# A fused FFT and mixture-of-experts kernel: the first two batches routed in halves, pauses between weight instructions on VectorE, and sums over partitions in bfloat16

## The chip, the cores and the metric

One core of a Trainium2 chip runs the whole program in one launch. The metric is the device time of that launch in microseconds, the median of several executions. The engines are named as the profile names them: PE (TensorE) multiplies matrices and PEld loads its weights, DVE (VectorE), ACT (ScalarE), POOL (GpSimd) and SP (SyncE) do the rest; each takes its instructions strictly in the order in which they stand in its queue.

## The reference

The input `x` is 8 batches of 2496 tokens by 256 features. Its two-dimensional Fourier transform, real part, is the input of a layer of 8 experts: each token goes to the expert with the largest logit.

```python
X = np.fft.fft(np.fft.fft(x, axis=1), axis=2).real      # 8 x 2496 x 256
x = X.reshape(19968, 256)
logits = x @ w_gate + modality_bias[modality_id]
e_idx = np.argmax(logits, axis=1)
gate_w = softmax(logits)[arange, e_idx]
for e in range(8):
    mask = e_idx == e
    h = np.maximum(x[mask] @ w1[e], 0.0)                 # 256 -> 1024
    out[mask] = gate_w[mask, None] * (h @ w2[e])         # 1024 -> 256
```

## The kernel before, in words

**Transform.** Each batch is loaded (`XM`, L368) and folded by DVE and ACT, goes through the three products of the transform on PE (`stage1` L523 or L520 in fp32 or fp16 form, `stage23` L554 or L549 and L569 or L567), and comes out of `evac` (L500 on ACT, L501 on DVE) as rows of 516 values in tiles `rp` of three groups of 128 tokens (`CH` = 3). A batch has 11 groups (`G` = 11). Half of the spectrum is enough: the mirrored rows `rm` are made from `rp` with a copy and a change of sign (`Group.rows`, L215, L217, L218). `Lg` (L577) collects the logits of each group.

**Routing.** `route(b)` (L609 to L684) runs on DVE behind the last group of a batch: logits, maximum, one-hot code, rank of each token within its expert (two kinds of small PE products, L653 and L655, and a running base `nbase`), and the destination `dsti` (L666). It works on all 22 columns (11 groups and their 11 mirrors) at once. It is a generator; the strings `ORDER0`, `ORDER1` give in which order its steps (`r`) alternate with steps of the next batch's `stage1` (`s`) and folds (`f`, `F`). The first three `r` steps have raised priority. The last of them makes the rows and for batches 0 and 1 issues at once their 22 indirect DMAs (`scatter`, L687, on POOL), which put each row at its place in `xd`, sorted by expert.

**Experts.** A block is 128 or 256 tokens of one expert. SP fetches it transposed (`xT`, L1038), PE makes the first product (L1054), ACT and DVE square off its two halves into `H` (L1059, L1060), PE makes the second product (L1072), ACT scales it (`ob`, L1078) and POOL writes it to its rows of the output with two indirect DMAs (L1079). The first three blocks (experts 0, 1, 2) are run as soon as batch 0 is in `xd`, 13 more when batch 1 is (`ORDER_S`); the rest follow batch by batch.

**Weights.** The fp32 weights of each expert (two units `u` per expert) are loaded (`wload`, L793), folded (L801, L802), measured (`wnorm`, L815, L817, L400), rounded to a scaled fp16 upper part by ACT (`whi`, L836) and a lower part by DVE (`wlo`, L843, four instructions of 128x1024 per expert), and stored (`wstore`, L851). `fft_moe` places these parts among the steps of the transform by hand with `steps(n)` and `behind(f, ins)`, the second at raised priority.

**Sums over partitions.** The scales are powers of two, taken from sums of squares: `total` (L400) multiplies a column of sums by a matrix of fp32 ones, `pow2` (L386 to L388) makes the power of two and its inverse.

**What sets the order.** A scheduler orders the instructions once, when the program is built, by priority, by `issue_after` and by the places where the source writes them; pools of tiles (`rt.tile(..., bufs=n)`) make a writer wait until the readers of the slot it takes over are done. Tiles `rp` of batches 0 to 2 have 6 slots (`RPB`), tiles `rm` 2 (`RMB`).

Of the kernel before, what the change touches and what calls it, by code (L numbers as in the profile page):

```python
# [34 lines left out]
RPB = 6  # L35
# [11 lines left out]
RMB = 2  # L47
# [39 lines left out]
ORDER1 = "rrrrrrrfssssFssss"  # L87
# [111 lines left out]
class Group:  # L199


    def __init__(self, k, b, g0, rp, tail, dsti):
# [31 lines left out]
class Kernel:  # L234
    def __init__(self, ctx, tc, t):
# [46 lines left out]
        self.ones = c.tile([P, P], F32, name="ones")  # L282
# [112 lines left out]
    def total(self, st, ps):  # L395
# [136 lines left out]
    def stage23(self, b):  # L532
# [8 lines left out]
        for g in range(G + 1):  # L541
# [67 lines left out]
    def route(self, b):  # L609
        nc, t, rt = self.nc, self.t, self.rt  # L610
        V, bc, be, tc = nc.vector, self.bc, self.be, self.tc
        Lg = self.Lg
        L = rt.tile([P, NC, 8], F32, name="L")
        V.tensor_tensor(L[:, 0:G, :], Lg[:, :, 0], Lg[:, :, 1], ALU.add)
        V.tensor_tensor(L[:, G:NC, :], Lg[:, :, 0], Lg[:, :, 1], ALU.subtract)
# [654 lines left out]
```

## Time and profile before

| what | us |
|---|---|
| three executions | 1132.57, 1125.27, 1128.35 |
| median | 1128.35 |
| the profiled execution | 1134.3 |
| its span, first to last instruction | 1132.5 |
| PE busy in it | 1028.2 |
| DVE busy in it | 561.6 |

All positions below are microseconds from the start of that span. A row of a timeline is start, duration, engine, line, operation, output and inputs, tile and count, and in brackets the idle time of the engine before it with what ended it. "Remote" and "another core or an unknown queue" stand for a signal whose sender the profile does not name; "issue" is idle time in which nothing shown was waited for. A row of the chain is start, duration and what ran or was waited for.

### The profile page before, as it was taken

The numbers are of one execution on the slowest core, as the hardware profiler recorded it, in microseconds if no ns is written. First come the engines' busy times: TensorE is split into PE (matmuls) and PEld (weight loads), VectorE is DVE, ScalarE is ACT, GpSimd is POOL, SyncE is SP. The second block draws the span as 40 slices with busy tenths as digits, with TensorE's granted clock in tenths as the row PEclk, the third lists the DMA queues.
The fourth block names the chain that finished last, engine by engine and source line by source line (L and its number), as shares of the span: only waits on it lengthen the run. The fifth ranks groups of instructions, "written<-read, shape, count | busy, mean of one in ns | idle before, by whom it ended". The sixth has DMA issues, their size and how long they took to land.

```text
span 1132.5 us, 26026 instructions
## 1 busy us (share of the span) xinstructions
PE 1028.2 (91%) x9980; PEld 913.4 (81%) x9980; DVE 561.6 (50%) x1645; ACT 441.0 (39%) x870; POOL 365.6 (32%) x351
## 2 busy tenths in 40 slices
PE   7954699987998699899999999999999999999997
PEld 6843489876897488698788989888888888899896
DVE  3638486968676368666456434642222222322231
ACT  4724174846552254443344333332232332323232
POOL 0156611146313232433433343244533221222111
PEclk9987799999999689899999999999999999999999
DMA  9465391668667568267766767388769898486963
GB/s 335 151 257 162 141 293 44 226 213 264 190 184 234 178 197 271 75 179 219 232 209 178 212 196 233 76 224 264 229 171 285 261 248 251 120 255 164 262 150 80
DMA packets 150011, 229.73 MB, mean 203 GB/s; under 512 B 116341, under 2 KB 117407, under 8 KB 132727
## 3 DMA queue, kind: packets, MB, share of 16 engines
q1 hardware_dynamic: 133319, 185.85, 57.3%
q0 software_dynamic: 16560, 42.15, 10.6%
q8 instruction: 80, 1.31, 0.5%
q14 instruction: 52, 0.43, 0.1%
HBM read 198.08 MB, written 62.48 MB: 230 GB/s over the span
## 4 chain that ended last, share of the span: by engine, by line
PE 61%; issue 14%; DVE 7%; DMA 6%; ACT 4%; another core or an unknown queue 4%; POOL 2%; ACTq 1%; SPq 0%; POOLq 0%; DVEq 0%
PE pso L1072 27%; PE psm L1054 26%; PE psf L549 2%; DMA XM<-x 2%; PE psf L567 2%; POOL out L1079 2%; DMA out<-ob,ig 2%; PE psf L554 1%; ACTq L1078 1%; PE psf L520 1%; DVE H L1060 1%; DVE w L843 1%; DMA pack<-c_pack 1%; DMA xd<-rm,dsti 1%
## 5 line engine op out<-in xcount | busy, mean ns | idle before, releaser
L1054 PE MATMUL psm<-xT,w 128*128 128x256 f16 (+1 forms) x4368 | 464.8, 263 | 35.9 <-issue 11.7
L1072 PE MATMUL pso<-w,H 128*128 128x256 f16 x3864 | 466.4, 276 | 20.5 <-issue 10.3
L1054 PEld LDWEIGHTS <-w 128*128 128x128 f16 x4368 | 386.6, 99 | 83.1 <-issue 38.3
L1072 PEld LDWEIGHTS <-H 128*128 128x128 f16 x3864 | 379.2, 99 | 73.5 <-issue 26.9
L1060 DVE SCALAR_TENSOR_TENSOR H<-psm,H 128x512 f16<-128x512 f32 x322 | 219.2, 686 | 299.4 <-ACT H L1059 244.2
L1079 POOL DMA_INDIRECT out<-ob,ig x161 | 162.1, 1007 | 625.7 <-ACT ob L1078 596.7
L1059 ACT ACTIVATE H<-psm 128x512 f16<-128x512 f32 x322 | 189.5, 597 | 280.8 <-PE psm L1054 199.7
L1078 ACT ACTIVATE ob<-pso,gs 128x256 f32<-128x256 f32 x161 | 69.4, 472 | 246.6 <-PE pso L1072 163.0
L687 POOL DMA_INDIRECT xd<-rp,dsti x88 | 102.8, 1169 | 84.1 <-ACT T L496 50.1
L687 POOL DMA_INDIRECT xd<-rm,dsti x88 | 92.0, 1045 | 48.5 <-issue 30.1
L501 DVE SCALAR_TENSOR_TENSOR T<-psf,T 120x280 f16<-120x280 f32 (+2 forms) x114 | 51.4, 462 | 56.3 <-ACT T L500 55.1
L500 ACT ACTIVATE T<-psf 120x280 f16<-120x280 f32 (+2 forms) x114 | 46.6, 424 | 38.2 <-PE psf L549 11.1
L1075 DVE TENSOR_SCALAR gs<-ig,w 128x2 f32<-128x2 f32 (+1 forms) x91 | 20.2, 223 | 72.3 <-DMA ig<-xd 44.6
L567 PE MATMUL psf<-T,pack 120*128 120x145 f16 (+1 forms) x396 | 41.5, 227 | 3.5 <-issue 1.6
L549 PE MATMUL psf<-pack,T 128*120 128x144 f16 (+1 forms) x396 | 40.2, 235 | 3.4 <-issue 3.1
L549 PEld LDWEIGHTS <-T 128*120 128x120 f16 x396 | 33.2, 137 | 3.6 <-issue 2.3
L567 PEld LDWEIGHTS <-pack 120*128 120x128 f16 x396 | 30.4, 99 | 7.1 <-issue 4.1
L501 DVE SCALAR_TENSOR_TENSOR rp<-psf,rp 128x256 f16<-128x256 f32 x66 | 27.4, 415 | 14.1 <-ACT rp L500 13.0
L520 PE MATMUL psf<-c,XM 128*128 128x132 f16 x360 | 28.7, 223 | 5.3 <-issue 3.3
L500 ACT ACTIVATE rp<-psf 128x256 f16<-128x256 f32 x66 | 25.3, 389 | 17.7 <-PE psf L567 11.0
L843 DVE SCALAR_TENSOR_TENSOR w<-wa,wsc,w 128x1024 f16<-128x1024 f32 x24 | 29.9, 1277 | 4.2 <-ACT w L836 4.2
L520 PEld LDWEIGHTS <-XM 128*128 128x128 f16 x360 | 23.9, 99 | 7.4 <-issue 4.1
(203 smaller groups left out, 621.2 us busy)
## 6 DMA issues: line engine op xcount, KB each, us to landing
w<-w SPq DMA_DIRECT2D x83, 1028.0 KB
w<-w SPq DMA_DIRECT2D x83, 1024.0 KB
XM<-x SPq DMA_DIRECT2D x14, 1280.0 KB
wa<-w SPq DMA_DIRECT2D x16, 1024.0 KB
out<-ob,ig POOLq DMA_INDIRECT x161
XM<-x SPq DMA_DIRECT2D x2, 768.0 KB
xT<-xd SPq DMA_TRANSPOSE x91
xd<-rp,dsti POOLq DMA_INDIRECT x88
```

The lines of the kernel that those rows point to most:

```text
L500: self.acted = self.nc.scalar.activation(dst[:, 0], ps, AF.Identity, scale=scale).ins
L501: self.mark = self.nc.vector.scalar_tensor_tensor(dst[:, 1], ps, scale, dst[:, 0], ALU.mult, ALU.subtract).ins
L520: nc.tensor.matmul(o, src[:, a, i0 + i, :], self.c1h[:, w, i1 + i, :], start=k == 0, stop=k == 2)
L549: nc.tensor.matmul(oh, T1[h][:, a, g, :], self.m2h[h][:, w], start=h + k == 0, stop=h * k == 2, skip_group_check=True)
L567: nc.tensor.matmul(ps3[0:P, cols], self.e3h[:, a, j, :], T2[:, w, cols], start=k == 0, stop=k == 2)
L687: i = self.nc.gpsimd.indirect_dma_start(out=self.t["xd"], out_offset=bass.IndirectOffsetOnAxis(ap=at, axis=0), in_=row, in_offset=None, bo ...
L1054: l1 = nc.tensor.matmul(ps[:, q, :], w1v[:, h, kt, ft], xT[:, xs, :], start=k == 0, stop=k == 5).ins
L1059: nc.scalar.activation(H[:, 0, f0:f0 + NF, :], ps, AF.Relu)
L1060: self.mark = V.scalar_tensor_tensor(H[:, 1, f0:f0 + NF, :], ps, 0.0, H[:, 0, f0:f0 + NF, :], ALU.max, ALU.subtract).ins
L1072: nc.tensor.matmul(po[:, tg, :], H[:, hh, ft, tg * P:(tg + 1) * P], w2v[:, wh, ft, :], start=k == 0, stop=k == 23)
L1078: self.ob = nc.scalar.activation(ob, po[:, tg, :], AF.Identity, scale=gs[:, tg:tg + 1]).ins
L1079: ins = nc.gpsimd.indirect_dma_start(out=t["out"], out_offset=bass.IndirectOffsetOnAxis(ap=ig.bitcast(I32)[:, tg, 0:1], axis=0), in_=ob, i ...
```

## The change

1. **Sums.** The ones are bfloat16. `total` multiplies the upper 16 bits of each fp32 sum, taken as bfloat16, and `pow2` multiplies the result by 1.01.
2. **Halves.** `route(b, ga, gb)` works on groups `ga` to `gb`. For batches 0 and 1 (`RH` = 2) it is called for groups 0 to 5 while `stage23` still makes groups 6 to 10 (three steps at group 6, then one for each group), and for groups 6 to 10 behind them. `ORDER0` and `ORDER1` have five `r` in place of seven, and two `steps` in `fft_moe` are shorter by two.
3. **Row tiles.** `rp` and `rm` of batches 0 to 2 share 8 slots.
4. **Pauses.** Behind each of the two low-part instructions of units 0 to 5 (`NG` = 6) `breathe` asks for four clears of one element per partition (`gap`, on 64 partitions), each to issue after the one before: 48 clears.

```diff
-RPB = 6
+RPB = 8
-RMB = 2
-ORDER0 = "rrrrrrrfssssFssss"
+ORDER0 = "rrrrrfssssFssss"
-ORDER1 = "rrrrrrrfssssFssss"
+ORDER1 = "rrrrrfssssFssss"
+RH = 2
+GH = 6
+RN0 = 3
+RG0 = 0
+NG = 6
+TR = 1.01
...
-    def __init__(self, k, b, g0, rp, tail, dsti):
+    def __init__(self, k, b, g0, rp, tail, dsti, ga, n):
+        self.c = [s * n + g0 - ga for s in range(2)]
...
-        pool, n = (k.rt, RMB) if self.b < SPB else (k.rows, RML)
-        rp, rm = rows = self.rp, pool.tile([P, CH, RW], I16, name="rm", bufs=n)
+        pool, n = (k.rt, RPB) if self.b < SPB else (k.rows, RML)
+        rp, rm = rows = self.rp, pool.tile([P, CH, RW], I16, name="rm", tag="row" if self.b < SPB else "rm", bufs=n)
...
+        self.gap = pk[64:P, 872:873]
-        self.ones = c.tile([P, P], F32, name="ones")
+        self.ones = c.tile([P, P], BF16, name="ones")
...
-        V.tensor_scalar(eb, ss, m, 1e-34, ALU.mult, ALU.max)
+        V.tensor_scalar(eb, ss, m * TR, 1e-34, ALU.mult, ALU.max)
...
-            nc.tensor.matmul(ps[:, 0:1], self.ones, st[:, i:i + 1], start=i == 0, stop=i == n - 1)
+            nc.tensor.matmul(ps[:, 0:1], self.ones, st.bitcast(BF16)[:, 2 * i + 1:2 * i + 2], start=i == 0, stop=i == n - 1)
...
-                    self.rp.append(pool.tile([P, CH, RW], I16, name="rp", bufs=n))
+                    self.rp.append(pool.tile([P, CH, RW], I16, name="rp", tag="rp" if pool is self.rows else "row", bufs=n))
...
-    def route(self, b):
+    def route(self, b, ga=0, gb=G):
+        n = gb - ga
+        m = 2 * n
...
-        nbase = rt.tile([P, 8], F32, name="nbase")
+        nbase = rt.tile([P, 8], F32, name="nbase", bufs=4)
...
-        self.base = self.bases[b + 1] = nbase
+        self.base = nbase
...
-        self.ntok += N
-        self.nbat = b + 1
+        if gb == G:
+            self.bases[b + 1] = nbase
+            self.ntok += N
+            self.nbat = b + 1
...
+                if b < RH and g >= GH:
+                    if g == GH:
+                        r = self.route(b, 0, GH)
+                        for _ in range(RN0):
+                            with self.hp(HR[min(b, 1)]):
+                                next(r)
+                    elif g > GH + RG0:
+                        next(r, None)
+            if b < RH:
+                for _ in r:
+                    pass
-            r, nr = self.route(b), 0
+            r, nr = self.route(b, GH) if b < RH else self.route(b), 0
...
+    def breathe(self, i):
+        for _ in range(4):
+            with self.tc.issue_after(i.ins):
+                i = self.nc.vector.memset(self.gap, 0.0)
...
-            V.scalar_tensor_tensor(o[:, 2 * F + m * i:2 * F + m * i + m], x, s, o[:, m * i:m * i + m], ALU.mult, ALU.subtract)
+            i = V.scalar_tensor_tensor(o[:, 2 * F + m * i:2 * F + m * i + m], x, s, o[:, m * i:m * i + m], ALU.mult, ALU.subtract)
+            if u < NG:
+                self.breathe(i)
...
-    steps(7)
+    steps(5)
     behind(both(k.wlo, 0, 1), k.head)
...
-    steps(4)
+    steps(2)
     behind(both(k.wlo, 4, 5), k.head)
```

What this does to the order of three places follows (a row is line, operation, output and inputs, shape, and a count where it repeats; lines of the new kernel are higher by some 20 to 40).

On POOL before, from the first scatter to the first writes of a block's output: the rows of batch 0 (22 scatters), of batch 1 (22), then block 0.

```order
L687 DMA xd<-rp,dsti 162048x516 x6
L687 DMA xd<-rm,dsti 162048x516 x3
L687 DMA xd<-rp,dsti 162048x516 x3
L687 DMA xd<-rm,dsti 162048x516 x3
L687 DMA xd<-rp,dsti 162048x516 x2
L687 DMA xd<-rm,dsti 162048x516 x5
L687 DMA xd<-rp,dsti 162048x516 x9
L687 DMA xd<-rm,dsti 162048x516 x3
L687 DMA xd<-rp,dsti 162048x516 x2
L687 DMA xd<-rm,dsti 162048x516 x8
L1079 DMA out<-ob,ig_1120 19968x256 x2
```

And now:

```order
L707 DMA xd<-rp,dsti 162048x516 x6
L707 DMA xd<-rm,dsti 162048x516 x6
L707 DMA xd<-rp,dsti 162048x516 x5
L707 DMA xd<-rm,dsti 162048x516 x5
L707 DMA xd<-rp,dsti 162048x516 x3
L707 DMA xd<-rm,dsti 162048x516 x3
L707 DMA xd<-rp,dsti 162048x516 x3
L707 DMA xd<-rm,dsti 162048x516 x3
L1117 DMA out<-ob,ig_1248 19968x256 x2
L707 DMA xd<-rp,dsti 162048x516 x5
L707 DMA xd<-rm,dsti 162048x516 x5
```

The rows come half by half, and the two output writes of block 0 have moved ahead of the last ten scatters of batch 1.

On DVE before, around the low parts of expert 0 (`w_0`):

```order
L891 SCALAR_TENSOR_TENSOR sp_nd_3_1104<-sp_ok_3_1096,done_99 1x3
L843 SCALAR_TENSOR_TENSOR w_0_104<-wf,wsc,w_0_104 128x1024
L843 SCALAR_TENSOR_TENSOR w_0_104<-wa,wsc,w_0_104 128x1024
L843 SCALAR_TENSOR_TENSOR w_0_107<-wa,wsc,w_0_107 128x1024 x2
L845 MEMSET w_0_107 128x7
L846 TENSOR_TENSOR w_0_107<-web 128x1
L600 TENSOR_TENSOR bias<-bias,btmp 128x176
```

And now:

```order
L929 SCALAR_TENSOR_TENSOR sp_nd_3_1232<-sp_ok_3_1224,done_99 1x3
L879 SCALAR_TENSOR_TENSOR w_0_104<-wf,wsc,w_0_104 128x1024
L839 MEMSET pack 64x1
L665 TENSOR_SCALAR tail<-gate,xinv 128x10
L879 SCALAR_TENSOR_TENSOR w_0_104<-wa,wsc,w_0_104 128x1024
L879 SCALAR_TENSOR_TENSOR w_0_107<-wa,wsc,w_0_107 128x1024 x2
L607 TENSOR_TENSOR bias<-bias,btmp 128x176
L394 TENSOR_SCALAR xeb<-xeb 128x1
L922 TENSOR_SCALAR sp_st_3_1226<-sp_st_3_1226 1x8
L883 MEMSET w_0_107 128x7
L884 TENSOR_TENSOR w_0_107<-web 128x1
```

One of the clears (MEMSET of `pack`, the tile that holds `gap`) and the last step of the first tail stand behind the first low part; the other three low parts stand back to back as before, and the clears that belong to them come later.

On DVE before, between batch 1's destinations and the low parts of expert 1 (`w_1`):

```order
L215 COPY rp<-tail 128x3x2
L215 COPY rm<-tail 128x3x2
L215 COPY rp<-tail 128x3x2
L217 COPY rm<-rp 128x3x2x129
L218 TENSOR_SCALAR rm<-rp 128x3x2x127
L215 COPY rp<-tail 128x2x2
L217 COPY rm<-rp 128x3x2x129
L218 TENSOR_SCALAR rm<-rp 128x3x2x127
L380 TENSOR_TENSOR XM<-XM 128x1280 x2
L843 SCALAR_TENSOR_TENSOR w_1_105<-wf,wsc,w_1_105 128x1024
L843 SCALAR_TENSOR_TENSOR w_1_105<-wa,wsc,w_1_105 128x1024
L843 SCALAR_TENSOR_TENSOR w_1_108<-wa,wsc,w_1_108 128x1024 x2
```

And now, between the second half's ranks of batch 1 and the same low parts:

```order
L1098 SCALAR_TENSOR_TENSOR H_1250<-psm,H_1250 128x512
L682 SCALAR_TENSOR_TENSOR dst<-pack,dst 128x10
L1098 SCALAR_TENSOR_TENSOR H_1250<-psm,H_1250 128x512
L917 TENSOR_SCALAR sp_ok_13_1735<-sp_av_1731 1x8
L660 TENSOR_REDUCE gate<-L 128x10
L917 TENSOR_SCALAR sp_ok_13_1747<-sp_av_1731 1x8
L684 CAST dsti<-dst 128x10
L387 TENSOR_TENSOR XM<-XM 128x1280 x2
L605 TENSOR_TENSOR bias<-mf,mb 128x176
L606 TENSOR_TENSOR btmp<-mid,mb 128x176
L879 SCALAR_TENSOR_TENSOR w_1_105<-wf,wsc,w_1_105 128x1024
L839 MEMSET pack 64x1
```

The copies for the mirrored rows no longer stand ahead of `XM` and `w_1`, and three of the `H` instructions of block 0 (L1098, before L1060; the first of the three stands a few rows higher) have moved ahead of them and of the destinations `dsti` of batch 1's second half.

## Rows read from the trace of the kernel before

**Rows 1.** The page, busy time and count of the engines, and the span in 40 slices of 28.3 us (busy tenths of PE, the granted clock of PE in tenths of full speed, the busy tenths of the DMA engines).

```profile
PE 1028.2 (91%) x9980; PEld 913.4 (81%) x9980; DVE 561.6 (50%) x1645; ACT 441.0 (39%) x870; POOL 365.6 (32%) x351
...
PE   7954699987998699899999999999999999999997
...
PEclk9987799999999689899999999999999999999999
DMA  9465391668667568267766767388769898486963
```

**Rows 2.** Windows: stretch, its length, busy time and count of PE, PEld, DVE, ACT, POOL, the granted clock of PE, the DMA share and GB/s.

```profile
68.00:81.00 13.00, 1.12 (x5) 0.62 (x4) 0.87 (x4) 1.20 (x4) 7.80 (x8) 0.74 0.63 242
81.00:93.00 12.00, 6.73 (x31) 5.37 (x32) 7.88 (x34) 7.09 (x12) 2.78 (x3) 0.78 0.09 31
93.00:102.00 9.00, 0.93 (x9) 0.67 (x8) 7.03 (x28) 1.98 (x4) 7.33 (x6) 0.50 0.43 106
102.00:135.00 33.00, 22.93 (x192) 18.68 (x191) 21.39 (x62) 7.05 (x13) 26.60 (x22) 0.81 0.63 212
...
250.00:300.00 50.00, 41.10 (x370) 35.37 (x369) 36.62 (x79) 32.59 (x53) 27.14 (x22) 0.97 0.84 251
900.00:1000.00 100.00, 100.00 (x918) 89.62 (x917) 28.25 (x50) 31.22 (x59) 19.46 (x20) 1.00 0.74 212
```

**Rows 3.** The timeline of PE.

```profile
80.72 1.30 PE L569 MATMUL psf<-T,pack 120*128 120x145 f32 x4 [11.88 <-ACT T L496]
...
101.36 5.78 PE L1054 MATMUL psm<-xT,w 128*128 128x256 f16 x36 [8.07 <-DMA xT<-xd]
...
274.95 2.21 PE L1054 MATMUL psm<-xT,w 128*128 128x256 f16 x12 [2.84 <-DVE H L1060]
```

**Rows 4.** The timeline of POOL.

```profile
51.21 1.12 POOL L687 DMA_INDIRECT xd<-rp,dsti  x1 [49.77 <-ACT T L496]
52.63 5.90 POOL L687 DMA_INDIRECT xd<-rp,dsti  x1 [0.30 <-ACT T L496]
...
77.09 0.97 POOL L687 DMA_INDIRECT xd<-rp,dsti  x1 [0.30 <-issue]
89.61 0.97 POOL L687 DMA_INDIRECT xd<-rm,dsti  x1 [11.55 <-DVE L L617]
...
94.75 0.97 POOL L687 DMA_INDIRECT xd<-rm,dsti  x1 [0.30 <-issue]
...
132.42 0.98 POOL L687 DMA_INDIRECT xd<-rm,dsti  x1 [0.30 <-issue]
133.70 0.98 POOL L1079 DMA_INDIRECT out<-ob,ig  x1 [0.30 <-issue]
```

**Rows 5.** The timeline of SP's queue.

```profile
98.02 0.70 SPq L1038 DMA_TRANSPOSE xT<-xd  x1
```

**Rows 6.** The timeline of DVE.

```profile
37.00 0.16 DVE L577 COPY Lg<-psf 128x16 f32<-128x16 f32 x1
...
43.27 0.25 DVE L614 TENSOR_TENSOR L<-Lg 128x88 f32<-128x88 f32 x1
...
43.72 0.34 DVE L617 TENSOR_TENSOR L<-L,bias 128x176 f32<-128x176 f32 x1
...
50.11 0.15 DVE L666 CAST dsti<-dst 128x22 int32<-128x22 f32 x1
...
53.69 3.66 DVE L843 SCALAR_TENSOR_TENSOR w<-wa,wsc,w 128x1024 f16<-128x1024 f32 x3
...
57.30 0.06 DVE L845 MEMSET w<- 128x7 uint32 x1
...
88.14 0.15 DVE L215 COPY rm<-tail 128x6 int32<-128x6 int32 x1
...
122.24 0.16 DVE L215 COPY rm<-tail 128x6 int32<-128x6 int32 x1 [1.52 <-DMA xd<-rm,dsti]
...
128.53 0.17 DVE L215 COPY rm<-tail 128x4 int32<-128x4 int32 x1 [4.86 <-DMA xd<-rm,dsti]
...
133.99 0.16 DVE L386 TENSOR_SCALAR web<-psf 128x1 f32<-128x1 f32 x1 [4.07 <-remote]
134.18 0.15 DVE L387 TENSOR_SCALAR web<-web 128x1 int32<-128x1 int32 x1
...
138.30 0.29 DVE L817 SCALAR_TENSOR_TENSOR wj<-psf,eye 128x128 bf16<-128x128 f32 x1 [3.59 <-remote]
```

**Rows 7.** Two stretches of the chain that ended last.

```profile
119.62 2.31 DMA xd<-rm,dsti
...
260.06 6.81 DMA xd<-rm,dsti
...
268.25 5.02 issue
```

**Rows 8.** The timeline of ACT.

```profile
130.49 0.84 ACT L1078 ACTIVATE ob<-pso,gs 128x256 f32<-128x256 f32 x2 [6.51 <-remote]
```

**Rows 9.** Windows of line L400 alone: stretch, its length, busy time and count of PE and of PEld, the clock, the DMA share and GB/s.

```profile
170.00:620.00 450.00, 8.68 (x60) 9.12 (x60) 0.94 0.64 194
```

**Rows 10.** Groups of line L400 by form, and the page's group of the fp16 weight loads of the experts' second product: for the first, count and the least, median and greatest ns of one, and the first and last start; for the second, count, busy time and mean ns of one.

```profile
L400 PEld LDWEIGHTS psf<-wst,ones x40: 190/192/338, 190.5 to 306.6; 128*128 128x128 f32 x40
...
L1072 PEld LDWEIGHTS <-H 128*128 128x128 f16 x3864 | 379.2, 99 | 73.5 <-issue 26.9
```

More of the change, by code (lines that the diff above doesn't have):

```diff
@@ L607, in be @@
         return v.unsqueeze(1).to_broadcast([P, NC, 8])
-    def route(self, b):
+    def route(self, b, ga=0, gb=G):
         nc, t, rt = self.nc, self.t, self.rt
[L611 to L615, printed above, removed]
+        V, tc = nc.vector, self.tc
+        n = gb - ga
+        m = 2 * n
+        two = lambda x: x.rearrange("p (s g) -> p s g", s=2)[:, :, ga:gb]
+        bc = lambda v: v.unsqueeze(2).to_broadcast([P, m, 8])
+        be = lambda v: v.unsqueeze(1).to_broadcast([P, m, 8])
+        by2 = lambda x: x.rearrange("p (s g) e -> p s g e", s=2)
+        Lg = self.Lg[:, ga:gb]
+        L = rt.tile([P, NC, 8], F32, name="L")[:, 0:m]
+        V.tensor_tensor(L[:, 0:n, :], Lg[:, :, 0], Lg[:, :, 1], ALU.add)
+        V.tensor_tensor(L[:, n:m, :], Lg[:, :, 0], Lg[:, :, 1], ALU.subtract)
+        bs = by2(self.bs)[:, :, ga:gb]
@@ L623, in route @@
         V.tensor_tensor(eq, L, bc(mx), ALU.is_equal)
         V.tensor_tensor(eq, eq, be(self.misc[:P, 8:16]), ALU.mult)
-        ix = rt.tile([P, NC], F32, name="ix")
+        ix = rt.tile([P, NC], F32, name="ix")[:, 0:m]
         V.tensor_reduce(ix, eq, AX.X, ALU.min)
-        V.scalar_tensor_tensor(ix, self.misc[:P, 24:46], 64.0, ix, ALU.mult, ALU.add)
+        bad = two(self.misc[:P, 24:46])
+        ix2 = ix.rearrange("p (s g) -> p s g", s=2)
+        V.scalar_tensor_tensor(ix2, bad, 64.0, ix2, ALU.mult, ALU.add)
@@ L642, in route @@
         yield
[L643 removed]
+        gate = rt.tile([P, NC], F32, name="gate")[:, 0:m]
         V.tensor_reduce(gate, L, AX.X, ALU.add)
@@ L652, in route @@
         o4f = o4.rearrange("p c e -> p (c e)")
-        nc.tensor.matmul(ps[:, 0:176], self.tri[:, 0, :], oh.rearrange("p c e -> p (c e)"), start=True, stop=False, skip_group_check=True)
-        for j in range(1, NC + 1, 4):
-            nc.tensor.matmul(ps[:, 8 * j:184], self.tri[:, 1, :], o4f[:, 0:184 - 8 * j], start=False, stop=j + 4 > NC, skip_group_check=True)
-        rk = rt.tile([P, NC, 8], F32, name="rk", bufs=1)
-        V.tensor_tensor(rk, ps[:P, 0:176].rearrange("p (c e) -> p c e", e=8), be(self.base[:P, :]), ALU.add)
@@ L658, in route @@
-        nbase = rt.tile([P, 8], F32, name="nbase")
-        V.tensor_tensor(nbase, ps[:, 176:184], self.base, ALU.add)
-        self.base = self.bases[b + 1] = nbase
+        w = 8 * m + 8
+        nc.tensor.matmul(ps[:, 0:8 * m], self.tri[:, 0, :], oh.rearrange("p c e -> p (c e)"), start=True, stop=False, skip_group_check=True)
+        for j in range(1, m + 1, 4):
+            nc.tensor.matmul(ps[:, 8 * j:w], self.tri[:, 1, :], o4f[:, 0:w - 8 * j], start=False, stop=j + 4 > m, skip_group_check=True)
@@ L672, in route @@
         yield
-        for i, g0 in enumerate(range(0, G, CH)):
-            group = Group(self, b, g0, self.rp[i], tail, dsti)
+        for g0 in range(ga, gb, CH):
+            group = Group(self, b, g0, self.rp[g0 // CH], tail, dsti, ga, n)
             if b < 2:
@@ L680, in route @@
             else:
-                self.pend += [(group, n) for n in range(2 * group.gn)]
-            if b == B - 1 and i == 3:
-                self.pend += [(self.pad, n) for n in range(E)]
+                self.pend += [(group, i) for i in range(2 * group.gn)]
+            if b == B - 1 and g0 == 9:
+                self.pend += [(self.pad, i) for i in range(E)]
             yield 1
```

37 lines of the change are left out of this document (20 added, 17 removed).

## The prediction

> **What bounds the kernel now**
>
> I read the page first. PE is busy for 1028.2 of 1132.5 us and its slices stand at 9 from the middle on, but there are holes in the first third [rows 1]. The windows put numbers on this: from 900 to 1000 us PE is busy for 100.00 of 100, while 68 to 81 holds 1.12 of 13, 81 to 93 6.73 of 12, 93 to 102 0.93 of 9, 102 to 135 22.93 of 33 and 250 to 300 41.10 of 50 [rows 2]. PE idles there for 11.88, 5.27, 8.07, 10.07 and 8.90 us. So the end is set by PE's work, and an edit gains only what it takes from these holes or from PE's work itself.
>
> Next I looked for what ends each hole. Three timelines answer for the early ones. PE waits 11.88 us to 80.72, then 8.07 us to 101.36 for the first fetched rows (DMA xT) [rows 3]. SP issues that fetch at 98.02 [rows 5], 3.27 us after the last scatter of batch 0 left POOL at 94.75 [rows 4]. That scatter is late because POOL idled 11.55 us before 89.61: the mirrored rows it needs are made on DVE from 88.14 [rows 6], behind batch 1's last row. From 102 to 138 DVE waits: 1.52 and 4.86 us for slots of `rm`, 4.07 and 3.59 us for a signal the profile calls remote [rows 6]. The chain has a landing of 2.31 us under the first wait, one of 6.81 us at 260, and 5.02 us of waiting before 273.27 [rows 7].
>
> **The change part by part**
>
> The sum is made against the profiled execution, 1134.3 us, which is 5.95 above the median of 1128.35; I take that off at the end.
>
> *Start of block 0.* Group 5's logits are ready at 37.00 against 43.27 for the start of routing now; routing then takes 6.84 us to `dsti` at 50.11 [rows 6]. So first destinations come at about 43.9 and the first scatter at 44.4, not 51.21. At the pitch of 1.28 us (132.42 to 133.70) and with the 4.9 us that one scatter lost (5.90 for about 1) [rows 4], twelve are out by 44.4 + 11 x 1.28 + 4.9 = 63.4, and ten more by 76.2. With the 6.61 us from the last scatter to PE's start now (94.75 to 101.36) block 0 could start at 82.8; PE has batch 1's transform to finish first, which ends at about 88 now, so I take 88, or 13.4 us earlier. Not all of this reaches the end. The work DVE does from 81 to 135 is 7.88 + 7.03 + 21.39 = 36.3 us of 54 [rows 2], which stays; only its 17.7 us of waits can go. Bounds 0 and 13.4; I take 4, about a third, because DVE's other work between 88 and 101 stays and now shares the engine with block 0's `H`.
>
> *Row slots.* With 8 shared slots the two waits for `rm`, 1.52 and 4.86 us, should go: gain 0 to 6.4, I take 5. Next late is then POOL itself, whose scatters are back to back. Batch 2's 5.02 us before 273.27 go in the same way, but only 2.84 us of that is PE idle (before 274.95) [rows 3]: 0 to 5, I take 3. Against that stands that `rp` now queues for the same slots; with all 22 scatters out by 76 it finds them free, and a wait there lies in the next item.
>
> *The hole from 68 to 81.* Nothing in the change removes its cause, which the rows leave unnamed. Scatters run through it now and will then. Some of PE's work may move across it: 0 to 5, I take 2.
>
> *The late signals, 4.07 and 3.59 us.* They sit in a run of scatters which now ends earlier. 0 to 7.7; I take half of it, 3.5.
>
> *Sums.* Line L400 holds PE for 8.68 us in 60 records between 170 and 620, 0.145 each [rows 9]. A sum is two such records and should become one, with a weight load of 99 ns as the page shows for fp16 in place of 192 [rows 10]. That is 30 x 0.145 = 4.3 us of PE, part of it inside holes: 0 to 8.7, I take 2.5.
>
> *Added work on DVE.* The trace has no chain of clears. A clear costs 0.06 us by the one at 57.30, or 0.19 by the pitch of instructions that wait for each other (133.99 to 134.18) [rows 6]: 48 cost 3 to 9 us. Halving a wide step costs 2 x 0.25 instead of 0.34 (43.27, 43.72), some 13 times in each of two batches, 4.2 us, and about as many short ones at 0.15 double, 4 us more. Most lies where DVE waits for ACT or PE, above all around 68 to 80: the run of clears stands there. Bounds 0 and -11 for what reaches the path; I take -5. `pow2` keeps its number of instructions: nothing.
>
> A scatter that normally takes 1 us took 5.90 beside the three low-part instructions at 53.69 [rows 4, 6]. The Trainium skill ("GPSIMD Engine Reference", section "Key points") says that GpSimd shares its SBUF interfaces with VectorE and contends with instructions that have two SBUF inputs, as these have; this trace agrees, with that 5.90. By that rule the pauses would give up to 4.9 us back to POOL. But the order puts one clear behind the first low part only, and three still run back to back, so I count none.
>
> Sum: 4 + 5 + 3 + 2 + 3.5 + 2.5 - 5 = 15 us. 1134.3 - 15 = 1119.3; on the median's basis 1113.4.
>
> **The rivals**
>
> *The early start is handed back.* DVE's queue now has `gs` and three `H` of block 0 ahead of batch 1's second destinations, so routing waits on PE where it waited on slots; the late signals stay. For it: the holes around 130 and 138 ended on signals that no slot explains [rows 6]. Against it: DVE is busy for 21.39 of 33 us from 102 to 135 [rows 2], so there is room. Left are row slots of batch 2 and sums, 3 + 2.5, and half of the clears' cost, -2.5: 3 us, 1125.4.
>
> *The holes close as well.* If what holds PE to 80.72 is the burst of scatters, and it moves ahead, the 11.88 us go but for the 2 counted, and the other 3.5 of the late signals: 9.9 + 3.5 more, 28 in all, 1100. For it: scatters stand beside both, at 77.09 and 132.42 [rows 4]. Against it: batch 1's 22 scatters, which end at 132.42, lie beside the 22.93 us that PE worked from 102 to 135 [rows 2, 4].
>
> *The pauses free POOL.* One scatter gains up to 4.9 us at block 0's start, a mechanism that lets the whole start come 4.9 earlier: 1108.5 if all of it counts. Against it is the order, above.
>
> *Slower: block 0's output writes hold up batch 1.* On POOL they now stand ahead of the last ten scatters, which go no earlier than `ob`. Before, `ob` came at 130.49 [rows 8], 29.1 us after block 0's start, and batch 1's last scatter at 132.42 [rows 4]. With `ob` at t the last scatter leaves at t + 12 x 1.28 = t + 15.4: the two are even at t = 117. From a start at 88 I get 88 + 29.1 - 6.4 = 110.7, and there is no harm. If block 0 still starts at 101.36 and takes as long, t is 130.5 and the last scatter 145.9, 13.5 us later, with 13 blocks behind it. Less 2.5 for the sums that is 11 us slower: 1139.4.
>
> **How the numbers follow**
>
> A measurement of this kernel can tell about 1%, 11.3 us, from no change. Forecast 0.55 (0.42 below 1117, 0.13 above); handed back 0.21; holes close 0.09; POOL freed 0.04; slower 0.11. Faster is 0.42 + 0.09 + 0.04 = 0.55, same 0.13 + 0.21 = 0.34, slower 0.11. The forecast's own range runs from 1105 to 1121. The range that should hold the time reaches into the closing holes below and past the handed-back case above, by about the 5 us of its DVE cost: 1098 to 1131.
>
> **What would show it right or wrong**
>
> The first scatter at 44 to 45 and the 22nd at 75 to 80; PE's first expert product at 84 to 92; no wait of a mirrored row on a scatter in batches 0 to 2; PE time of the sums halved; a hole of about 10 us still somewhere from 62 to 85; clears of 0.06 to 0.19 us each. The forecast is wrong if block 0 starts after 95, if POOL idles for over 5 us before its two output writes, if the hole near 68 is gone, or if DVE takes the place of the slots by standing at `gs` or `H` for over 5 us.

## The result, and the profile after

The changed kernel is slower: 1134.97 us, median of 19 executions (1130.38 to 1148.24), against 1126.77 for the kernel before (19 executions, 1115.91 to 1132.89). The ratio is 1.0094, with a 95% interval of 1.0067 to 1.0121; it counts only the executions within 1.5% of the fastest of their kernel, while the medians of all 19 stand to each other as 1.0073. So the loss is 8 to 11 us, just under the 1% that the prediction took for the least that can be told from no change. The forecast was 1113.4 with a range from 1098 to 1131.

The profiled execution of the changed kernel took 1130.74 us, with a span of 1128.9. It lies at the lower end of its 19, while the profiled execution of before, 1134.3, lies above the 19 that it is compared with. So the two traces cannot show the loss as a difference of spans. They show where the gain that was forecast did not come.

Windows of the changed kernel, columns as in [rows 2]:

```profile
68.00:81.00 13.00, 1.39 (x14) 1.02 (x12) 4.88 (x35) 2.50 (x7) 5.86 (x7) 0.67 0.78 310
81.00:93.00 12.00, 10.94 (x61) 9.04 (x61) 9.04 (x43) 5.74 (x12) 2.92 (x3) 0.79 0.36 76
93.00:102.00 9.00, 2.42 (x24) 1.86 (x21) 1.69 (x8) 2.92 (x3) 6.81 (x7) 0.88 0.47 120
102.00:135.00 33.00, 22.91 (x174) 17.92 (x175) 26.72 (x88) 7.79 (x14) 7.68 (x8) 0.77 0.43 154
135.00:170.00 35.00, 24.42 (x220) 19.13 (x218) 24.92 (x75) 20.81 (x37) 10.90 (x11) 0.85 0.73 221
```

PE idles for 11.61, 1.06, 6.58, 10.09 and 10.58 us, 39.9 in all. Before, the same five stretches hold 11.88, 5.27, 8.07 and 10.07 [rows 2] and, from 135 on, 4.51:

```profile
135.00:170.00 35.00, 30.49 (x284) 25.79 (x284) 26.08 (x58) 22.14 (x41) 5.18 (x5) 0.94 0.87 245
```

That is 39.8 in all. The holes from 81 to 102 shrank by 5.7 us, and the one from 135 on grew by 6.1.

POOL of the changed kernel, answering to [rows 4]:

```profile
45.14 1.18 POOL L707 DMA_INDIRECT xd<-rp,dsti  x1 [43.70 <-DVE rm L224]
...
74.71 0.97 POOL L707 DMA_INDIRECT xd<-rm,dsti  x1 [0.31 <-issue]
89.41 0.97 POOL L707 DMA_INDIRECT xd<-rp,dsti  x1 [13.72 <-ACT rp L507]
...
103.46 0.97 POOL L707 DMA_INDIRECT xd<-rm,dsti  x1 [0.30 <-issue]
124.31 0.97 POOL L1117 DMA_INDIRECT out<-ob,ig  x1 [19.88 <-ACT ob L1116]
...
130.93 0.97 POOL L707 DMA_INDIRECT xd<-rp,dsti  x1 [3.73 <-DVE rm L221]
...
142.59 0.97 POOL L707 DMA_INDIRECT xd<-rm,dsti  x1 [0.30 <-issue]
```

The first scatter goes at 45.14 (51.21 before) and the 22nd at 74.71 (94.75 before). Batch 1's first 12 run from 89.41 to 104.4. The ten of its second half, however, start at 130.93 and end at 143.6; before, all of batch 1 was out at 133.4. PE and DVE, answering to [rows 3] and [rows 6], show what lies between:

```profile
90.80 4.09 PE L1092 MATMUL psm<-xT,w 128*128 128x256 f16 x36
...
94.80 0.23 PE L672 MATMUL psf<-o,tri 128*128 128x80 f16 x3
95.98 0.39 PE L1110 MATMUL pso<-w,H 128*128 128x256 f16 x2 [0.95 <-ACT H L1097]
108.04 2.74 PE L1092 MATMUL psm<-xT,w 128*128 128x256 f16 x12 [11.67 <-DVE H L1098]
```

```profile
94.67 0.23 DVE L655 TENSOR_TENSOR L<-L,mx 128x80 f32<-128x80 f32 x1
106.81 0.24 DVE L674 TENSOR_TENSOR rk<-psf,nbase 128x80 f32<-128x80 f32 x1 [11.91 <-remote]
...
107.32 0.67 DVE L1098 SCALAR_TENSOR_TENSOR H<-psm,H 128x512 f16<-128x512 f32 x1
...
109.71 0.15 DVE L684 CAST dsti<-dst 128x10 int32<-128x10 f32 x1
...
130.51 0.14 DVE L221 COPY rp<-tail 128x6 int32<-128x6 int32 x1
```

PE starts block 0 at 90.80, 10.6 us sooner than before. It has started the rank products of batch 1's second half (L670, L672) by 94.80, but DVE gets to add to them (`rk`, L674) only at 106.81, after 11.91 us on a signal called remote. The chain that ended last passes through this wait:

```profile
94.90 11.88 another core or an unknown queue
106.81 0.24 DVE rk L674
```

Behind `rk` in DVE's queue stand block 0's `H`, so PE waits for those until 108.04, then `dsti` (109.71), then `XM` and expert 1's low parts, and only at 130.51 the row copies that free the last ten scatters. The ranks are not the only ones that wait here. ACT makes its half of `H` ahead of DVE's, and it too stood on remote signals:

```profile
102.44 0.60 ACT L1097 ACTIVATE H<-psm 128x512 f16<-128x512 f32 x1 [6.51 <-remote]
106.75 0.60 ACT L1097 ACTIVATE H<-psm 128x512 f16<-128x512 f32 x1 [3.71 <-remote]
```

So the second and third `H` of DVE could not have come before about 103 and 107 (an estimate from these rows) even without the ranks; only the first hangs on them alone.

The waits on remote signals, whole span: engine and line that waited, total, times, longest. First the changed kernel, then before.

```profile
ACT H L1097 <- remote: 60.6, 16, 10.8
...
DVE rk L674 <- remote: 11.9, 1, 11.9
```

```profile
ACT H L1059 <- remote: 37.7, 10, 11.8
...
ACT ob L1078 <- remote: 13.1, 2, 6.6
```

All of them add up to 96.7 us in 28 waits after the change, and to 91.8 in 24 before. The two at 134 and 138 that the prediction names are among these 24.

The sums' windows and loads, answering to [rows 9] and [rows 10]:

```profile
170.00:620.00 450.00, 3.79 (x30) 2.71 (x30) 0.95 0.66 198
```

```profile
L407 PEld LDWEIGHTS <-ones x48: 95/97/152, 13.3 to 584.1; 128*128 128x128 bf16 x48
```

Their PE time between 170 and 620 fell from 8.68 to 3.79 us, and a weight load from 192 to 97 ns.

### The profile page after: what moved, and what is told of

The parts are those of the page before. It is cut to its first block, busy times and chain, and to the rows that moved or that the text cites. A ratio compares the mean times of both kernels' runs of the same rounds, so it can differ in the third digit from the quotient of the medians.

```text
span 1128.9 us, 26025 instructions
## 1 busy us (share of the span) xinstructions
PE 1022.3 (91%) x9934; PEld 904.2 (80%) x9934; DVE 572.4 (51%) x1741; ACT 440.9 (39%) x872; POOL 351.9 (31%) x351
## 4 chain that ended last, share of the span: by engine, by line
PE 66%; issue 13%; DVE 9%; another core or an unknown queue 3%; ACT 2%; POOL 2%; DMA 2%; SPq 1%; POOLq 0%; DVEq 0%; ACTq 0%
PE psm L1092 29%; PE pso L1110 28%; PE psf L574 2%; PE psf L556 2%; POOL out L1117 2%; PE psf L527 2%; PE psf L561 2%; DVE w L879 2%; DVE H L1098 1%; DMA pack<-c_pack 1%; SPq L1076 1%; PE psf L576 1%; DMA wa<-w 1%; DVE rp L508 1%
## 5 line engine op out<-in xcount | busy, mean ns | idle before, releaser
L1092 PE MATMUL psm<-xT,w 128*128 128x256 f16 (+1 forms) x4368 | 469.6, 264 | 35.8 <-DVE H L1098 14.8
L1110 PE MATMUL pso<-w,H 128*128 128x256 f16 x3864 | 463.1, 275 | 17.2 <-issue 10.6
L1098 DVE SCALAR_TENSOR_TENSOR H<-psm,H 128x512 f16<-128x512 f32 x322 | 218.8, 687 | 308.3 <-ACT H L1097 228.4
L1117 POOL DMA_INDIRECT out<-ob,ig x161 | 159.4, 990 | 648.5 <-ACT ob L1116 615.8
L707 POOL DMA_INDIRECT xd<-rp,dsti x88 | 93.1, 1058 | 87.4 <-DVE rm L224 44.0
```

The lines of the kernel that those rows point to most:

```text
L707: i = self.nc.gpsimd.indirect_dma_start(out=self.t["xd"], out_offset=bass.IndirectOffsetOnAxis(ap=at, axis=0), in_=row, in_offset=None, bo ...
L1092: l1 = nc.tensor.matmul(ps[:, q, :], w1v[:, h, kt, ft], xT[:, xs, :], start=k == 0, stop=k == 5).ins
L1098: self.mark = V.scalar_tensor_tensor(H[:, 1, f0:f0 + NF, :], ps, 0.0, H[:, 0, f0:f0 + NF, :], ALU.max, ALU.subtract).ins
L1110: nc.tensor.matmul(po[:, tg, :], H[:, hh, ft, tg * P:(tg + 1) * P], w2v[:, wh, ft, :], start=k == 0, stop=k == 23)
L1117: ins = nc.gpsimd.indirect_dma_start(out=t["out"], out_offset=bass.IndirectOffsetOnAxis(ap=ig.bitcast(I32)[:, tg, 0:1], axis=0), in_=ob, i ...
```

## The experiments

Every series compares its kernels with before in alternating executions. Before itself took 1137 us in the first series, 1075 in the second, third and fourth, and 1129 in the fifth. The traces differ with it: those of series one and five have 23 to 36 waits on remote signals (72 to 141 us), those of the other three have none at all, in any kernel. The runs don't say what makes these waits; they were not put in by any edit. The record names another chip for each series (5, 10, 1, 2 and 12, in this order; for the result it names none), so chip and time changed together, and no run tells which of the two brings the waits. Ratios are to before of the same series.

| kernel | ratio, 95% interval | remote waits, us | block 0 starts | last scatter of batch 1 |
|---|---|---|---|---|
| changed (the result) | 1.0094 (1.0067 to 1.0121) | 96.7 | 90.80 | 142.59 |
| e1, no clears | 1.0073 (1.0035 to 1.0111) | 109.0 | 92.98 | 143.45 |
| e2, fp32 sums | 1.0002 (0.9969 to 1.0036) | 105.3 | 97.99 | 137.79 |
| e3, batch 0 alone in halves | 1.0048 (1.0015 to 1.0082) | 141.4 | 96.00 | 132.11 |
| e4, no halves | 1.0109 (1.0072 to 1.0146) | 111.8 | 97.17 | 146.70 |
| e7, before with bfloat16 sums | 0.9978 (0.9958 to 0.9999) | 0 | 95.34 | 127.72 |
| e10, halves and slots only | 0.9967 (0.9944 to 0.9990) | 0 | 85.57 | 117.74 |
| e8, rows ahead of expert 1 | 0.9929 (0.9907 to 0.9951) | 0 | 87.53 | 120.13 |
| e5, before with paced scatters | 1.0109 (1.0082 to 1.0136) | 0 | 102.03 | 139.76 |
| e11, changed | 0.9954 (0.9937 to 0.9972) | 0 | 85.85 | 126.56 |
| e12, before | 1.0013 (0.9990 to 1.0037) | 0 | 92.70 | 120.26 |
| e13, as e8 | 0.9945 (0.9910 to 0.9980) | 0 | 89.70 | 122.29 |
| e14, as e5 | 1.0119 (1.0082 to 1.0155) | 0 | 102.00 | 140.10 |
| e16, changed | 0.9960 (0.9937 to 0.9983) | 0 | 87.84 | 128.51 |
| e17, batch 1's later routing steps at raised priority | 0.9953 (0.9934 to 0.9973) | 0 | 87.47 | 129.30 |
| e18, as e10 | 0.9954 (0.9927 to 0.9982) | 0 | 86.37 | 121.89 |
| e19, as e4 | 1.0030 (0.9994 to 1.0067) | 72.1 | 94.92 | 144.50 |
| e20, as e2 | 0.9990 (0.9951 to 1.0029) | 117.9 | 97.79 | 137.42 |
| e21, as e3 | 0.9983 (0.9946 to 1.0020) | 81.8 | 90.31 | 126.42 |

**First series: one part undone each.** The first theory was that the halves cost the time.

e1 leaves out the clears:

```diff
-NG = 6
+NG = 0
```

> The changed kernel without the 48 clears (NG = 0), all else kept. Theory H (the halves cost the time, because batch 1's second half comes 10 us late): the time stays within 4 us of the changed kernel's 1135, some 0.5 to 1% over the kernel before. Rival C (the clears cost it): 48 clears of 0.1 to 0.19 us give back 5 to 9 us, 1126 to 1130, no slower than before.

e2 goes back to fp32 sums:

```diff
-TR = 1.01
+TR = 1.0
...
-        self.ones = c.tile([P, P], BF16, name="ones")
+        self.ones = c.tile([P, P], F32, name="ones")
...
-            nc.tensor.matmul(ps[:, 0:1], self.ones, st.bitcast(BF16)[:, 2 * i + 1:2 * i + 2], start=i == 0, stop=i == n - 1)
+            nc.tensor.matmul(ps[:, 0:1], self.ones, st[:, i:i + 1], start=i == 0, stop=i == n - 1)
```

> The changed kernel with fp32 ones and fp32 sums as before (no factor 1.01). The trace gives the sums 13.9 us of PE before and 5.8 after, 4.9 of the difference between 170 and 620 us. If PE's time for the sums reaches the end: 3 to 8 us slower than the changed kernel, about 1140. If it lies in PE's holes: no difference, 1135. If the bfloat16 sums are what makes the change slow: 1125.

e3 routes batch 1 whole:

```diff
-RH = 2
+RH = 1
-ORDER1 = "rrrrrfssssFssss"
+ORDER1 = "rrrrrrrfssssFssss"
...
-    steps(2)
+    steps(4)
```

> The changed kernel with only batch 0 routed in halves (RH = 1; ORDER1 and the second shortened steps as before). Theory H: block 0 still starts at 88 to 92, batch 1's last scatter comes at 130 or earlier instead of 143, and the 10 us come back: 1120 to 1127. Rival C: batch 1 makes no difference, 1131 to 1137.

e4 routes batch 0 whole as well (`RH = 0`, `ORDER0` with seven `r` and `steps(7)` beside the edits of e3):

```diff
-RH = 2
+RH = 0
```

> The changed kernel with both batches routed whole (RH = 0; both orders and both steps as before); clears, bfloat16 sums and the 8 shared row slots stay. Theory H: block 0 starts at about 100 again, the sums and the slots gain 3 to 8 us over the kernel before, the clears take some of it: 1118 to 1127. Rival C: still 1131 to 1137.

The first theory missed: it had e3 and e4 level with before or faster, and they were 0.5 and 1.1% slower. Without any halves (e4) the kernel was as slow, so in this series the halves are not the cause as such. Only fp32 sums (e2) brought it back to before, though they add work to PE. The orders gave a second theory, O: the scheduler knows the sums as shorter and orders much else anew; with bfloat16 sums it puts the row copies of batch 1's second half behind expert 1's low parts and block 1's first `H`.

**Second series: the sums alone, the rows first, and scatters paced.**

e7 is the kernel before with the bfloat16 sums:

```diff
-        self.ones = c.tile([P, P], F32, name="ones")
+        self.ones = c.tile([P, P], BF16, name="ones")
...
-        V.tensor_scalar(eb, ss, m, 1e-34, ALU.mult, ALU.max)
+        V.tensor_scalar(eb, ss, m * 1.01, 1e-34, ALU.mult, ALU.max)
```

with `total` as in the change.

> The kernel before with the bfloat16 sums alone (with the factor 1.01). In its order block 0's two output writes stand ahead of batch 1's last five scatters and one copy of mirrored rows stands behind expert 1's weights, which the shorter sums alone bring about in the scheduler. Theory O (the sums cost time by the order that they bring): 0.3 to 1% slower than before, batch 1's last scatter some 5 us later. Rival A (only their arithmetic counts, 4 to 5 us of PE between 170 and 620): 0.2 to 0.5% faster than before.

e10 joins the edits of e1 and e2 (`NG = 0` and fp32 sums).

> The changed kernel with fp32 sums and without clears: halves and shared slots are left. It is e1 with fp32 sums. In its order the rows of batch 1's second half stand ahead of expert 1's weights, and the output writes of block 0 behind all scatters. Theory O: 0.7% below e1, so level with before or up to 0.5% faster, batch 1's last scatter at 130 to 136. If the halves themselves cost time: still 0.5% slower than before or more.

e8 moves expert 1's low parts behind the rows:

```diff
-    steps(3)
-    behind(both(k.wlo, 2, 3), k.head)
+    steps(5)
+    behind(both(k.wlo, 2, 3), k.head, k.rowed)
...
-    steps(2)
+    steps(0)
     behind(both(k.wlo, 4, 5), k.head)
```

> The changed kernel with the low parts of expert 1 issued only after the rows of batch 1's second half are made (two steps of the transform moved ahead of them). Sums, clears, halves and slots stay. The rows then stand ahead of expert 1's weights, as with fp32 sums, but behind a part of blocks 0 and 1. Theory O: some of the loss comes back, 0.2 to 0.7% slower than before instead of 0.9%. If the place of the rows doesn't matter: 0.9% slower, or more, since expert 1's weights come later.

e5 is the kernel before with a clear on POOL between any two scatters of batches 0 and 1:

```diff
     def scatter(self, row, at, b):
+        x = ExitStack()
+        if b < 2 and self.paced:
+            x.enter_context(self.tc.issue_after(self.paced))
...
+        x.close()
         self.scatter_dep(i, b)
         self.scattered = i.ins
+        if b < 2:
+            with self.tc.issue_after(i.ins):
+                self.paced = self.nc.gpsimd.memset(self.padrow[:, 0:512], 0).ins
```

> The kernel before with a clear of 128 x 512 int16 on POOL behind each scatter of batches 0 and 1 (0.5 us by the clear of padrow, so a pitch of about 2 us in place of 1.28). Theory B (a run of scatters at the pitch of 1.28 us holds back PE's signals to ACT and DVE): the hole of 11.9 us at 68 to 81 and the late signals at 130 to 138 shrink to under half, while batch 0's last scatter stays within 5 us of before; the time falls by up to 1%. Rival (the transfers of weights and x that fill the queues cause the hole, or the number of scatters does): the holes stay, and the time grows by the later scatters, up to 1%.

Theory O missed on e7: the sums alone were 0.2% faster, though they do move block 0's writes ahead of five scatters. It missed on e8 too, which it had 0.2 to 0.7% slower and which was 0.7% faster. e10 and e8 were faster than before, where e1 and the changed kernel had been slower. Either those edits help, or the missing remote waits do. e5 cost 1.1%; its trace had no remote waits to take away, so it says nothing on theory B.

**Third series: the changed kernel and before themselves.**

> The changed kernel unchanged, once more, beside before on one chip. Where the trace has waits on signals that it calls remote (92 us in 24 waits in the first profile of before, 97 in 28 of after), theory R (those late signals hold back the routing of batch 1's second half, whose ranks now wait on PE beside the first half's scatters) expects 0.5 to 1.2% slower than before, batch 1's last scatter at 140 to 146. Where the trace has none (as in the four runs of the last series), the ranks do not wait and it expects level with before to 0.6% faster, last scatter at 120 to 135. Theory O (the place of the rows alone) expects 0.5% slower or more in either.

> The kernel before, once more, for its trace beside the changed one on one chip: ratio 1. With remote waits: holes of 10 to 12 us at 66 to 81, 1120 to 1140; without: 1070 to 1080, the hole at 66 to 81 under 6 us.

> The changed kernel with expert 1's low parts only behind the rows of batch 1's second half (0.7% faster than before in the last series, where no wait was on a remote signal). Theory O: 0.4 to 0.8% below the changed kernel on the same chip, whichever kind of trace. Theory R: where remote waits are there the gain over before is gone, ratio 1.000 to 1.008, and the changed kernel is as slow; where there are none, the changed kernel is as fast as this, within 0.3%.

> The kernel before with a clear on POOL behind each scatter of batches 0 and 1, as e5 (1.1% slower where no remote waits were). Theory B (scatters at the pitch of 1.28 us cause the remote waits): where before has them, they shrink to under half in the first 140 us, and the kernel is level with before or faster. Rival: they stay, and the kernel is slower by 1% or more as in e5.

This answers one part. The changed kernel, unaltered, is 0.46% faster than before here, so its order alone does not make it slower. DVE and POOL of e11 at the place where the changed kernel stood still:

```profile
89.77 0.23 DVE L655 TENSOR_TENSOR L<-L,mx 128x80 f32<-128x80 f32 x1
90.17 0.24 DVE L674 TENSOR_TENSOR rk<-psf,nbase 128x80 f32<-128x80 f32 x1 [0.17 <-PE psf L672]
...
93.41 0.15 DVE L684 CAST dsti<-dst 128x10 int32<-128x10 f32 x1
```

```profile
82.72 0.97 POOL L707 DMA_INDIRECT xd<-rp,dsti  x1 [8.06 <-ACT T L503]
...
92.94 0.97 POOL L707 DMA_INDIRECT xd<-rp,dsti  x1 [0.31 <-issue]
...
114.67 0.97 POOL L707 DMA_INDIRECT xd<-rp,dsti  x1 [3.74 <-DVE rm L221]
...
126.56 1.11 POOL L707 DMA_INDIRECT xd<-rm,dsti  x1 [0.30 <-issue]
```

The ranks waited 0.17 us where they had waited 11.91, `dsti` came at 93.41 in place of 109.71, and the last ten scatters began at 114.67 in place of 130.93. The rows stand behind expert 1's low parts as before, so theory O's order is there and the loss is not. That the ranks' wait makes the loss where remote waits are (theory R) is not shown by this: every remote wait of the kernel is gone here, not this one alone. e13, with the rows ahead, is level with e11 (0.9945 and 0.9954). e14 repeats e5.

**Fourth series: three variants beside one another.**

> The changed kernel, once more, beside two of its variants. With remote waits in its trace: 0.5 to 1.2% slower than before. Without: 0.3 to 0.7% faster, as in e11.

e17 does not repeat the edit of e8 and e13. It raises the priority of batch 1's later routing steps:

```diff
-                    with self.hp(HR[min(b, 1)] if nr <= HRN else 0):
+                    with self.hp(HR[min(b, 1)] if nr <= (9 if b == 1 else HRN) else 0):
```

> The changed kernel with expert 1's low parts behind the rows of batch 1's second half. With remote waits, theory O (the place of the rows behind expert 1's weights is what costs time) expects it 0.4 to 0.9% below the changed kernel; theory R (the wait of the ranks on PE costs it, whatever stands behind) expects the two within 0.3%. Without remote waits: as in e8 and e13, 0.5 to 0.7% faster than before, and level with the changed kernel.

> The halves and the shared slots alone (fp32 sums, no clears). With remote waits, theory O expects it level with before or faster (its rows stand ahead of expert 1's weights), theory R 0.3 to 1% slower. Without remote waits: as e10, 0.3% faster than before.

No remote waits again, and all three are 0.4 to 0.5% faster than before and level with one another. But e17's edit does not do what its expectation says. On DVE the row copies of batch 1's second half still stand behind expert 1's low parts, at 115.86 (116.22 in e16, but 107.61 in e13, ahead of them):

```profile
99.82 3.69 DVE L879 SCALAR_TENSOR_TENSOR w<-wa,wsc,w 128x1024 f16<-128x1024 f32 x3
115.86 0.22 DVE L221 COPY rp<-tail 128x6 int32<-128x6 int32 x2
```

So e17 is the changed kernel's order once more and says nothing on the place of the rows; e8 and e13 alone do. e18 lacks the clears and the bfloat16 sums: both together move nothing that can be measured there.

**Fifth series: the first again.**

> As e4: both batches routed whole; sums, clears and slots as changed. It was the slowest of its series (1.011 of before, with remote waits); block 0's output writes stand ahead of all 22 scatters of batch 1 there. Theory R (late remote signals set what the order costs): with remote waits 1.005 to 1.015 again; without, 0.995 to 1.002. Theory O (the place in POOL's queue costs it by itself): 1.005 to 1.011 in either.

> As e2: halves, slots and clears with fp32 sums (1.000 of before, with remote waits). Theory R: without remote waits 0.993 to 0.998, like the changed kernel, so the sums' place in the order stops mattering; with them 0.997 to 1.004. Theory O: 0.3% or more below the changed kernel in either, so 0.992 or less without remote waits.

> As e3: only batch 0 in halves (1.005 of before, with remote waits). Without remote waits theory R expects 0.993 to 0.999; if the halves of batch 1 are what gains there, 0.999 to 1.002.

Remote waits were back, and with them before at 1129 us. But e4's 1.0109 became 1.0030 and e3's 1.0048 became 0.9983. Where these waits are, a ratio thus moves by up to 0.8% between two series, more than its interval says, and the ranking within the first series is not to be built on. Neither theory had e19 right: both expected at least 0.5% slower with these waits, and it was 0.3%, with before inside its interval. What held in all: none of the variants gained clearly where the waits are, while every one with halves gained where they are not.

Two things in these two series speak against the ranks' wait as the whole cause. First, e2 and e20 meet it too and are level with before, though block 0 starts later in them (a row of e2, then one of e20):

```profile
114.75 0.24 DVE L674 TENSOR_TENSOR rk<-psf,nbase 128x80 f32<-128x80 f32 x1 [5.78 <-remote]
114.44 0.24 DVE L674 TENSOR_TENSOR rk<-psf,nbase 128x80 f32<-128x80 f32 x1 [9.66 <-remote]
```

Second, e4 loses time although its ranks do not wait. What e1, e4, e19 and the changed kernel share is that block 0's output writes stand ahead of scatters of batch 1, and POOL stands 19.65, 27.10, 24.78 and 19.88 us for them; they are at 1.0030 to 1.0109. In e2, e3, e20 and e21 the writes stand behind all scatters, and POOL waits 0.31 to 3.34 us for them; they are at 0.9983 to 1.0048, below the others of their series. No run moves the writes alone, and the intervals of the two groups overlap in part, so this is a rival and not shown.

## Why the prediction was wrong

**Right: the early half.** First scatter at 45.14 (44.4 forecast; the prediction's own rows, 37.00 + 6.84 + 1.10, give 44.9), 22nd at 74.71 (76.2), block 0 at 90.80 (88). No mirrored row of batch 1 waits for a slot any more. A clear takes 0.06 us (53.07, below), and in a run of ten 0.11 each, between the two prices:

```profile
162.20 1.13 DVE L839 MEMSET pack<- 64x1 f32 x10
```

**Wrong: what the early half is worth.** "Start of block 0" (4), "row slots" of batch 1 (5) and "late signals" (3.5) were to take 12.5 us out of PE's holes by 170. Measured: 39.8 us of holes before, 39.9 after. Before 68, PE stands for 12.91 us in place of 9.56, 3.35 more, which the prediction has nowhere but in DVE's added work. The step that failed is the one on the late signals. I took them as tied to two places, 134 and 138, halved them because the scatters there would end sooner, and charged nothing for new ones. But the trace of before holds 24 of them, and the hole from 68 to 81, whose cause the prediction left unnamed, hangs on two of them, 10.96 us and then 2.42 us of ACT:

```profile
77.39 0.47 ACT L500 ACTIVATE rp<-psf,xsc 128x256 f16<-128x256 f32 x1 [10.96 <-remote]
```

After the change they are as long in all (96.7 us for 91.8) and stand at other instructions. The first half's 12 scatters run from 89.41 to 104.4, the second half's ranks fall right into them, and DVE, which takes its work in order, stands for 11.91 us with block 0's `H` and the second half's destinations behind. That is as much as the 10.6 us won at block 0's start; that the one cancels the other is read from this trace and not shown by an experiment, and with ACT's two waits of the same stretch the ranks can carry only a part.

The 3 us of batch 2's slots went the same way. DVE no longer waits for a slot there, but ACT stands for 10.85 us on a remote signal, and PE idles for 8.75 us from 250 to 300 where it idled for 8.90:

```profile
250.00:300.00 50.00, 41.25 (x336) 32.08 (x335) 31.11 (x79) 23.85 (x40) 22.08 (x21) 0.83 0.70 215
```

```profile
276.61 0.60 ACT L1097 ACTIVATE H<-psm 128x512 f16<-128x512 f32 x1 [10.85 <-remote]
```

The sign I named for this, DVE standing "at `gs` or `H` for over 5 us", was one instruction off: it stood at `rk`, whose wait I had not listed among the waits that the halves add. Another sign that I named came true as it stands: POOL idled for over 5 us, 19.88, before its two output writes.

**The rival "handed back"**, 3 us of gain, had late signals staying; they did. Without remote waits it is right in kind: block 0 starts 6.85 us earlier in e11 than in e12, yet PE's holes from 68 to 170 fall only from 23.1 to 21.5 us, and the whole gain is 0.46% of 1074, 5 us. The windows of e12 and of e11:

```profile
81.00:93.00 12.00, 1.27 (x9) 0.94 (x10) 9.24 (x38) 1.62 (x3) 9.26 (x10) 0.50 0.38 110
...
102.00:135.00 33.00, 26.84 (x251) 23.03 (x250) 24.70 (x72) 16.34 (x27) 20.46 (x17) 0.95 0.72 231
135.00:170.00 35.00, 35.00 (x359) 31.87 (x358) 26.64 (x59) 18.48 (x39) 4.88 (x5) 1.00 0.60 179
```

```profile
81.00:93.00 12.00, 10.78 (x72) 8.92 (x72) 7.85 (x36) 7.78 (x12) 7.84 (x9) 0.83 0.56 133
...
102.00:135.00 33.00, 25.26 (x237) 20.65 (x236) 30.13 (x106) 16.90 (x29) 15.89 (x14) 0.95 0.73 256
135.00:170.00 35.00, 31.64 (x324) 27.70 (x322) 25.93 (x71) 16.80 (x37) 4.58 (x4) 1.00 0.64 165
```

Of the 9.5 us won from 81 to 93, 4.9 come back from 102 to 170 (6.16 us of holes there in e12, 11.10 in e11) and 3.0 from 68 to 81 and 93 to 102. So "start of block 0" and "row slots", 9 us together, came to 1.6 us of holes even where no signal is late: these terms were too large too.

**The slower rival** happened in part, and its 1139.4 is the number nearest to 1134.97. Its point was `ob` at 117; `ob` let the writes go at 124.31, so the queue held the last ten scatters. But POOL then stood 3.73 us more for the row copies, which came at 130.51: DVE's order was the later of the two. Its premise, a late start of block 0, did not hold: block 0 started at 90.80, but `ob` came only at 123.56, since PE stood still from 96.4 to 108.04. The first and fifth series, above, leave this rival open.

**Sums.** They gave 4.9 us of PE time from 170 to 620, near the 4.3 worked out. In the end time e7, the sums alone, was 0.2% faster, about the 2.5 us forecast but hardly clear of nothing; e18 beside e16 shows no gain, but lacks the clears as well. The sums also order the program anew, which I had not looked for; e7 does not show that this costs time.

**Added work on DVE.** The bounds of 0 and -11 take the clears at 3 us; with the 9 that the prediction also gives, the lower one is -17. No run shows the -5 by itself: where e16 and e18 differ by clears and sums together, they are level.

**The low parts and POOL.** The prediction read one scatter of 5.90 us; one row was too little to go by. In the changed kernel the scatter that meets the first low part takes 2.13 us and ends at 53.86, behind the clear at 53.07; those beside the three low parts that stand back to back take 0.97 to 1.26. Before, the one scatter there took 5.90 [rows 4]. What the Trainium skill ("GPSIMD Engine Reference", section "Key points") says of instructions with two SBUF inputs holds for the first of these scatters and not for the later ones. But e1, without clears, took 2.19 and 2.48 there, so the clear is not shown to be the reason:

```profile
51.75 1.27 DVE L879 SCALAR_TENSOR_TENSOR w<-wf,wsc,w 128x1024 f16<-128x1024 f32 x1
53.07 0.06 DVE L839 MEMSET pack<- 64x1 f32 x1
...
53.30 3.69 DVE L879 SCALAR_TENSOR_TENSOR w<-wa,wsc,w 128x1024 f16<-128x1024 f32 x3
```

```profile
51.73 2.13 POOL L707 DMA_INDIRECT xd<-rp,dsti  x1 [0.31 <-issue]
54.17 1.26 POOL L707 DMA_INDIRECT xd<-rm,dsti  x1 [0.30 <-issue]
55.73 0.97 POOL L707 DMA_INDIRECT xd<-rm,dsti  x1 [0.31 <-issue]
```

**Open.** What makes the remote waits, chip or time or something else, and theory B with it, since the paced kernel met none. Whether the loss, where they are, comes from the ranks' wait, from the place of block 0's writes on POOL, or from both. Before lost 52 us from the third series to the result (1074.4 to 1126.8), the changed kernel 65 (1069.6 to 1135.0), but the trace shows one execution near the fast end, whose early part is level with before. And whether the 0.94% itself would repeat in another series with remote waits: the changed kernel was timed once there.

## What to carry to other kernels

Before counting a step that starts earlier, follow the first wait that is now behind it on an engine that works in order: here the ranks of batch 1, which had waited for nothing, were moved into the stretch where signals came late. A wait that the profile cannot name is not a fixed cost of its place; ask which instruction of the new order will stand there. And run both kernels in several series and on several chips, since a sign can turn with conditions that neither kernel sets. Last, read an experiment's trace to see that the edit did what it was made for: e17's did not.

## What the runs showed of the hardware that was not expected

The same kernel took 1075 us in three series and 1127 to 1137 in three others, and the traces of the slower ones carry 23 to 36 waits on remote signals where the faster ones have none. In all nine traces with such waits, the first stands behind the first scatter into `xd` (77.39 behind 51.2 in before) and the last ahead of the end of the last (833.71 ahead of 880.3, the rows that pad `xd`); the transform's last logits are copied at 717.2 in before, so the waits outlast it, and the output writes go on behind both. That the waits keep to the time of the scatters does not show that the scatters make them. Some stand beside runs of scatters 1.28 us apart (94.67 to 106.81 above, where DMA moved 120 GB/s from 93 to 102), but e11's scatters from 82.72 to 93.9 have the same pitch and no such wait: the pitch alone does not bring them.
